# Nine attention transposes of units 8 to 12 done by SyncE's transfers instead of TensorE, and one output copy done by ScalarE instead of VectorE

## The chip, the cores and the metric

The kernel runs on one core of one Trainium2 chip. The metric is the device time of one execution in microseconds; lower is better. Before the change the median of three runs is 290.44 us (289.84 to 291.09).

## The reference

A sliding-window attention over 8 batches of 8 heads, 576 positions and 64 dimensions is followed by a feed-forward block over the resulting 4608 tokens of width 512, with a hidden width of 2048 and a gelu approximated by a sigmoid. The output is float32.

```python
def _attn_ref(q, k, v):
    ...
    window = 32
    scale = 1.0 / np.sqrt(D)
    scores = scale * np.matmul(q, k.transpose(0, 1, 3, 2))
    pos = np.arange(S)
    mask = np.abs(pos[:, None] - pos[None, :]) <= window
    scores = np.where(mask, scores, -1000000000.0)
    ...                                   # softmax over the last axis
    return np.matmul(attn, v).astype(np.float32)

def _moe_ref(x, w_in, w_out):
    h = x @ w_in
    g = h * (1.0 / (1.0 + np.exp(-1.702 * h)))
    return (g @ w_out).astype(np.float32)
```

## The kernel before

The 4608 tokens are cut into 36 units of 128 keys and into nine tiles of 512 tokens, four units to a tile. Everything is written out by hand in program order: each engine executes its instructions in the order in which the program issues them, and waits on semaphores that the framework sets from the buffers used.

A unit passes through these steps. GpSimd's transfers load its queries, keys and values and turn them into bfloat16 (`fetch`, `load_kq`, `load_v`; the queries and keys go to the staging buffers `qst` and `kst`, five of each). Queries and keys are transposed so that the head dimension lies on the partitions (`qT`, `kT`, seven buffers of each, handed out by `place`). TensorE multiplies them (`scores`), ScalarE takes the exponential (line 256), VectorE applies the band mask (`band`), TensorE multiplies by the values (`values`), VectorE divides (`norm`), and the result `x` is transposed again into `xT`, the right operand of the first layer. The values are also needed shifted by half a unit; GpSimd makes that copy (`odd_v`, lines 209 and 210).

How queries and keys are transposed depends on the unit. Units 0 to 7 are transposed on TensorE by two routines of their own. Keys 8 to 12 and queries 8 to 11 are transposed on TensorE by `T_pe`: four transposes of 128x128 for each, three operands at a time into the two banks "t", and ScalarE copies each to its place. From query 12 and key 13 on, `turn` has SyncE issue a transfer that transposes (`T_dma`, line 223). The transposes of `x` are also SyncE's transfers from tile 3 on (line 306); the output stores stand in the same queue (line 453). At most eight transfers of a queue are under way: each waits for the one eight before it.

The feed-forward block of tile 0 is computed plainly (`layer1_plain`, `layer2_plain`); the later tiles use seven products in place of eight for a 2x2 block product. For the first layer that is `l1_group`, four groups to a tile. A group's seven products are issued in the order P1, P7, P6, P2, P5, P4, P3 into four banks A, C, B, E. ScalarE copies A to B, and C to `s7`, after P1 and P7; P6 adds to B; VectorE writes E = B + s7 (line 432) and, after P5 has added to B, C = B + s7 (line 438); then come four gelus (line 419). Between the products, `fill` puts in matmuls of the second layer of the tile before and work for VectorE: sums of weights (`w1_sums`, `w2_sums`, lines 335 and 346) and sums of the hidden layer (`g_sums`, lines 366 to 369).

The change concerns the first layer of tile 1, `first_layer1`, from 48 to 70 us of the span. Its fills hold the plain second layer of tile 0: two halves of 32 matmuls each, whose two banks LA and LB are copied out at the last of their 16 matmuls (line 475). In this stage the transposes of `T_pe` stand after P7 of groups 1, 2 and 3, and GpSimd loads units 12 to 15. Ahead of it, at the end of `opening`, stand the scores of unit 7, which still read the keys at the start of unit 8 from a buffer of the opening.

Of the kernel before, what the change touches and what calls it, by code (L numbers as in the profile page):

```python
# [16 lines left out]
BF16 = mybir.dt.bfloat16  # L17
# [9 lines left out]
class _Kernel:  # L27
# [191 lines left out]
    def T_dma(self, c, u):  # L219
# [1 line left out]
            return  # L221
        src = self.stage.pop((c, u))
        self.nc.sync.dma_start_transpose(self.place(c, u), src.rearrange("p h d -> p (h d)"))

    def T_pe(self, which, eng):

        tp = self.bank("t", [128, 4, 4, 128], BF16, "tp")
        which = [(x[0], int(x[1:])) for x in which]
        for i, (c, u) in enumerate(which):
            src = self.stage.pop((c, u)).rearrange("p h d -> p (h d)")  # L230
            for hp in range(4):
                self.nc.tensor.transpose(tp[:, i, hp, :], src[:, 128 * hp:128 * hp + 128], self.ident)  # L232
        for i, x in enumerate(which):
            self.copy(eng, self.place(*x), tp[:, i])

    def scores(self, u, tag):
        kT, q = self.kT[u], self.qT[u]
# [224 lines left out]
    def layer2_plain(self, t, pr):  # L464

        st = {}

        def part(i, f):
            if not st:
                st.update({j: self.bank("L" + "AB"[j], name="o") for j in range(2)})  # L470
                st["o"] = self.sb("o_sb", [128, 2, self.DM], F32, 2)
            lo = 256 * i + 128 * pr
            self.mm(st[i], self.g[t][:, f, lo:lo + 128], self.w2[:, f, :], start=(f == 0))
            if f == 15:
                self.copy((self.nc.vector, self.nc.scalar)[i * pr], st["o"][:, i, :], st[i])
                if i == 1:
                    self.store(t, pr, st["o"])

        return [lambda i=i, f=f: part(i, f) for q in range(8) for i in range(2) for f in (2 * q, 2 * q + 1)]
# [82 lines left out]
    def opening(self):  # L562

        nc, dve, act, pool = self.nc, self.nc.vector, self.nc.scalar, self.nc.gpsimd
        self.setup()
        dve.memset(self.idle, 0.0)
        dve.memset(self.spark, 0.0)
        for t in self.ve:
            dve.memset(t[:, :, self.D:], 1.0)
        self.load_first("k", 0)  # L570
        self.load_first("q", 0)
        make_identity(nc, self.ident)
        act.activation(self.spark, self.spark, AF.Exp)
        for u in (0, 1, 2):
            self.load_v(u)
        self.load_w1(0)
        self.setup_mask()
        self.load_first("k", 1)
        self.load_first("q", 1)
        self.cut_mask()  # L580
        self.load_w1(1)
        self.load_v(3)
        self.load_v(4)
        self.load_w1(2)
        self.load_four("k")
        self.load_four("q")
        self.load_w1(3)
        dve.tensor_copy(self.identh, self.ident)
        self.keep_busy(20, "E")
        self.T_first("k", 0, "AC", (dve, act))  # L590
        self.keep_busy(6, "E")
        self.T_first("q", 0, ("LA", "LB"), (dve, act))
        self.keep_busy(4, "E")
        for u in (5, 6):
            self.load_v(u)
        self.load_w2(0)
        for u in (7, 8):
            self.load_v(u)
        for c in (1, 2, 3):
            self.load_w2(c)  # L600
        self.load_kq("k", 8)
        self.scores(0, "t")
        self.scores(1, "AC")
        self.odd_v(0, dve)
        self.odd_v(1, dve)
        self.keep_busy(10, "E")
        self.band(0)
        self.band(1)
        self.values(0, "t")
        self.values(1, "AC")  # L610
        self.norm(0)
        self.norm(1)
        self.keep_busy(6, "E")
        self.x_T(0, "LA", act)
        self.keep_busy(4, "E")
        self.x_T(1, "LB", act)
        self.T_first("k", 1, "AC", (dve, dve))
        h, n, gelus = [], [0], []

        def l1(half, *ds):  # L620
            for d in ds:
                self.layer1_plain(0, d, half, h[n[0] % len(h)])
                n[0] += 1

        self.layer1_plain(0, 0, 0, "B", gelus)
        self.T_first("q", 1, ("LA", "LB"), (dve, act))
        self.layer1_plain(0, 1, 0, "E", gelus)
        self.odd_v(2, dve)
        self.odd_v(3, dve)
        h[:] = ["LB", "B", "E"]  # L630
        self.scores(2, "t")
        self.scores(3, "AC")
        self.layer1_plain(0, 2, 0, "LA", gelus)
        self.layer1_plain(0, 3, 0, "LB", gelus)
        self.do(gelus)
        self.band(2)
        self.band(3)
        self.values(2, "t")
        self.norm(2)
        self.values(3, "AC")  # L640
        self.norm(3)
        self.x_T2(2, "A", dve)
        l1(0, 4)
        dve.tensor_copy(self.k_first, self.kT[0][:, :, 0:64])
        dve.tensor_copy(self.v_first, self.ve[0][0:64])
        for u in (8, 9, 10, 11):
            self.fetch(u)
        l1(1, 0, 1)
        halo = self.kT[4]
        self.T_four("k", "AC", (dve, dve))  # L650
        dve.tensor_copy(self.kT[4][:, :, 0:64], halo)
        l1(1, 2, 3)
        l1(0, 5)
        self.T_four("q", "AC", (dve, act))
        l1(1, 4, 5)
        self.odd_v(4, dve)
        self.scores(4, "t")
        self.scores(5, "AC")
        for i in (3, 1, 2, 4):
            self.w1_sums((i,), 0)  # L660
        self.odd_v(5, dve)
        for d, tag in ((6, "B"), (7, "E")):
            self.layer1_plain(0, d, 0, tag, gelus)
        self.do(self.l2, 3)
        self.scores(6, "t")
        self.do(self.l2, 3)
        self.scores(7, "AC")
        self.do(gelus)
        self.do(self.l2, 2)
        self.band(4)  # L670
        self.band(5)
        self.odd_v(6, dve)
        self.odd_v(7, dve)
        self.band(6)
        self.values(4, "t")
        self.norm(4)
        self.band(7)
        self.values(5, "AC")
        self.norm(5)
        self.do(self.l2, 8)  # L680
        self.values(6, "t")
        self.norm(6)
        self.values(7, "AC")
        self.norm(7)
        h[:] = "BE"
        n[0] = 0
        for i in (3, 1):
            self.w1_sums((i,), 1)
        l1(1, 6, 7)
        self.x_T2(4, "A", act)  # L690
        self.do(self.l2, 4)
        self.x_T2(6, "t", dve)
        self.do(self.l2, 4)
# [147 lines left out]
    def first_layer1(self):  # L841

        dv = [lambda i=i: self.w1_sums((i,), 1) for i in (2, 4)]
        for n in range(4):
            if n == 3:
                self.turn(12)
                self.turn(13)
            self.odd_v(8 + n, self.nc.gpsimd)
            self.fetch(12 + n)

            def fill(i):
                self.do(self.l2, {1: 1, 7: 1, 2: 3, 4: 3}[i])
                self.do(dv, {1: 2, 7: 1, 2: 0, 4: 2}[i] if n else 0)
                if i == 7 and n:
                    self.T_pe([("k8", "q8", "k9"), ("q9", "k10", "q10"), ("k11", "q11", "k12")][n - 1], self.nc.scalar)

            self.l1_group(1, n, fill, lambda i: self.do(dv, 1))
            dv += self.g_sums(1, 2 * n, 2)
            if n in (0, 1):
                dv += [lambda i=i, j=j: self.w2_sums((i,), j) for i in ((3, 1), (2, 4))[n] for j in range(2)]  # L860
        return dv
# [46 lines left out]
```

## Time and profile before

| | |
|---|---|
| median of three runs | 290.44 us |
| lowest, highest run | 289.84, 291.09 us |
| span of the profiled execution, first to last instruction | 287.4 us |
| granted TensorE clock over the span | 1.000 |
| VectorE, ScalarE, GpSimd busy share of the span | 75%, 68%, 44% |
| transfers | 37.63 MB in 148074 packets |

The profile is of one execution. The page gives its span, not a time of its own; the runs' median lies 3.0 us above that span. Busy shares are averages over all stages, so a question about one place is asked of the rows of that place: a timeline gives start and length in us of each instruction, or of a run of equal ones, with their count, and in brackets how long the engine was idle before it and what it then waited for. The chain of waits lists the work that ended last, followed back from the end.

### The profile page before, as it was taken

The page shows a single profiled execution, that of the slowest core. Times are in us where ns is not written, and L with a number is a line of the kernel's source. Part 1 is how long each engine was busy: PE and PEld are TensorE (multiplying, and loading weights), DVE is VectorE, ACT ScalarE, POOL GpSimd, SP SyncE. Part 2 cuts the span into 40 slices and gives each one's busy share as a digit, 9 for nine tenths or more (in the row PEclk, how much of TensorE's full clock was granted, in tenths as well). Part 3 has the DMA queues.
Part 4 walks back from the last instruction along what each step waited for, and adds up shares of the span by engine and source line. Part 5 has one row for each costly group of instructions (what it writes and reads, how often), then busy time and mean ns, then how long its engine had stood idle before and what let it go on. Part 6 is the DMA issues. An engine that isn't in the chain of part 4 may idle for free.

```text
span 287.4 us, 9107 instructions
## 1 busy us (share of the span) xinstructions
PE 274.7 (96%) x3762; PEld 227.1 (79%) x3762; DVE 216.9 (75%) x501; ACT 194.0 (68%) x340; POOL 127.3 (44%) x192
## 2 busy tenths in 40 slices
PE   7878999999999997999999999999999999999995
PEld 5666857776777885888788888888888888888884
DVE  1756898897887975798779887988797878946731
ACT  2455784789787767676967696679668965558421
POOL 8964448798599746456345826360210000000000
PEclk9999999999999999999999999999999999999999
DMA  8999999999999999999999999998432150401023
GB/s 94 186 192 197 184 204 156 190 116 140 168 141 148 175 142 173 138 203 144 188 97 181 161 168 105 173 135 146 95 77 45 69 112 0 94 2 73 2 92 130
DMA packets 148074, 37.63 MB, mean 131 GB/s; under 512 B 134976, under 2 KB 143680, under 8 KB 148032
## 3 DMA queue, kind: packets, MB, share of 16 engines
q0 software_dynamic: 104464, 18.42, 92.3%
q1 hardware_dynamic: 43120, 18.10, 36.0%
q8 instruction: 29, 0.48, 0.7%
q10 hardware_dynamic: 448, 0.52, 0.6%
q14 instruction: 13, 0.11, 0.1%
HBM read 36.83 MB, written 9.44 MB: 161 GB/s over the span
## 4 chain that ended last, share of the span: by engine, by line
PE 81%; DMA 5%; DVE 5%; ACT 3%; POOL 2%; issue 2%; DVEq 0%; ACTq 0%; POOLq 0%
PE h L70 38%; PE o L70 34%; PE pv L70 3%; DMA xT<-x 3%; PE sc L70 2%; DMA kq<-in_k_dram 2%; DVE x L294 2%; ACT p L256 1%; PE tp L322 1%; POOL ve L199 1%; ACT L256 1%; DVE p L264 1%; PE tp L189 1%; PE tp L232 1%; ACT g L419 1%
## 5 line engine op out<-in xcount | busy, mean ns | idle before, releaser
L419 ACT ACTIVATE g<-h 128x512 f16<-128x512 f32 x128 | 72.1, 598 | 35.8 <-PE h L70 35.0
L70 PEld LDWEIGHTS <-g 128*128 128x128 f16 x576 | 54.4, 98 | 11.4 <-issue 1.8
L70 PEld LDWEIGHTS <-a 128*128 128x128 f16 x512 | 49.1, 97 | 12.7 <-DVE xs L354 2.1
L70 PE MATMUL h<-xs,a 128*128 128x256 f16 x384 | 57.6, 272 | 1.2 <-DVE xs L354 0.9
L70 PE MATMUL o<-w,g 128*128 128x256 f16 (+1 forms) x320 | 55.3, 294 | 0.9 <-issue 0.8
L70 PEld LDWEIGHTS <-w 128*128 128x128 f16 x512 | 49.1, 98 | 7.8 <-issue 1.2
L70 PE MATMUL h<-xT,w 128*128 128x256 f16 x384 | 54.0, 273 | 1.1 <-issue 1.0
L199 POOL DMA_DIRECT2D ve<-in_v_dram x40 | 34.0, 855 | 40.7 <-issue 33.7
L70 PEld LDWEIGHTS <-gs 128*128 128x128 f16 x384 | 36.8, 98 | 5.2 <-issue 0.4
L256 ACT ACTIVATE p<-sc 128x512 bf16<-128x512 f32 x72 | 36.6, 619 | 3.2 <-PE sc L70 3.2
L70 PE MATMUL o<-b,gs 128*128 128x256 f16 x256 | 37.8, 273 | 1.0 <-issue 0.5
L70 PE MATMUL o<-b,g 128*128 128x256 f16 x256 | 37.3, 273 | 0.0
L432 DVE TENSOR_TENSOR h<-h,s 128x512 f32<-128x512 f32 x32 | 22.3, 698 | 18.2 <-PE h L70 18.2
L131 POOL DMA_DIRECT2D qst<-in_q_dram x35 | 28.1, 805 | 5.5 <-DMA w<-in_moe_w_out_dram 3.2
L131 POOL DMA_DIRECT2D kst<-in_k_dram x31 | 26.4, 854 | 8.5 <-DMA ve<-in_v_dram 2.6
L67 ACT COPY h<-h 128x512 f32<-128x512 f32 x32 | 18.6, 581 | 16.6 <-PE h L70 16.2
L294 DVE TENSOR_TENSOR x<-pv,rec 128x256 f16<-128x256 f32 (+1 forms) x53 | 27.6, 520 | 1.8
L438 DVE TENSOR_TENSOR h<-h,s 128x512 f32<-128x512 f32 x32 | 22.4, 700 | 5.1 <-PE h L70 4.6
L264 DVE TENSOR_TENSOR p<-p,mask 128x1024 bf16<-128x1024 bf16 x36 | 24.6, 685 | 0.9 <-ACT p L256 0.8
L209 POOL COPY vo<-ve 64x264 int32<-64x264 int32 x28 | 13.4, 480 | 24.9 <-PE pv L70 23.8
L67 ACT COPY s<-h 128x512 f32<-128x512 f32 x32 | 19.1, 596 | 3.0 <-PE h L70 1.8
L70 PE MATMUL h<-xs,w 128*128 128x256 f16 x128 | 19.2, 273 | 0.0
(85 smaller groups left out, 361.1 us busy)
## 6 DMA issues: line engine op xcount, KB each, us to landing
out_dram<-o_sb SPq DMA_DIRECT2D x33, 256.0 KB, 3.9
ve<-in_v_dram POOLq DMA_DIRECT2D x32, 128.0 KB, 6.3
kst<-in_k_dram POOLq DMA_DIRECT2D x25, 128.0 KB, 6.8
qst<-in_q_dram POOLq DMA_DIRECT2D x21, 128.0 KB, 6.1
w<-in_moe_w_in_dram POOLq DMA_DIRECT2D x4, 512.0 KB, 8.9
w<-in_moe_w_out_dram POOLq DMA_DIRECT2D x4, 512.0 KB, 13.4
qst<-in_q_dram POOLq DMA_DIRECT2D x7, 96.0 KB, 5.5
kq<-in_q_dram POOLq DMA_DIRECT2D x2, 256.0 KB, 5.9
```

Of the source, the lines that this page charges most:

```text
L67: (eng.copy if eng is self.nc.scalar else eng.tensor_copy)(out, in_)
L70: self.nc.tensor.matmul(out, lhsT, rhs, start=start, stop=stop, skip_group_check=True)
L131: self.nc.gpsimd.dma_start(t[off:off + n], src[b, :, s:s + n, :].rearrange("h s d -> s h d"))
L189: self.nc.tensor.transpose(tp[64 * (h % 2):64 * (h % 2) + 64, h // 2, j, :], src[:, 4 * i + h, j, :], self.ident)
L199: self.nc.gpsimd.dma_start(t[off:off + n, :, :self.D], self.v[b, :, s:s + n, :].rearrange("h s d -> s h d"))
L209: eng.tensor_copy(words(vo[64:128]), words(self.ve[u % 9][64:128]))
L256: self.nc.scalar.activation(p[:, eo].rearrange("k h s -> k (h s)"), sc[eo], AF.Exp, scale=self.scale)
L264: (eng or self.nc.vector).tensor_mul(pv, pv, msk.to_broadcast([128, 8, 2, SQ]))
L294: dve.tensor_mul(x[:, 4 * at:4 * (at + n), :].rearrange("p (b h) d -> p b h d", b=n), acc[:, :, :, :D], r.to_broadcast([128, n, 4, D]))
L419: act.activation(g[:, f, 256 * half:256 * half + 256], bank.rearrange("p (i n) -> p i n", i=2), AF.Gelu_apprx_sigmoid)
L432: dve.tensor_add(e, b, s7)
L438: dve.tensor_add(c, b, s7)
```

## The change

The routine `T_pe` and its calls go. Keys 8 to 10 and queries 8 and 9 are transposed by SyncE's transfers, issued behind the scores of unit 7; query 10 and key 11 at the start of group 1 of `first_layer1`, query 11 and key 12 at the start of group 2. In the plain second layer of tile 0, the copy of the second bank goes to ScalarE in both halves; before, it did so in the second half alone.

```diff
-    def T_pe(self, which, eng):
-
-        tp = self.bank("t", [128, 4, 4, 128], BF16, "tp")
-        which = [(x[0], int(x[1:])) for x in which]
-        for i, (c, u) in enumerate(which):
-            src = self.stage.pop((c, u)).rearrange("p h d -> p (h d)")
-            for hp in range(4):
-                self.nc.tensor.transpose(tp[:, i, hp, :], src[:, 128 * hp:128 * hp + 128], self.ident)
-        for i, x in enumerate(which):
-            self.copy(eng, self.place(*x), tp[:, i])
...
             if f == 15:
-                self.copy((self.nc.vector, self.nc.scalar)[i * pr], st["o"][:, i, :], st[i])
+                self.copy((self.nc.vector, self.nc.scalar)[i], st["o"][:, i, :], st[i])
...
         self.scores(7, "AC")
+        self.T_dma("k", 8)
+        for u in (8, 9):
+            self.turn(u)
         self.do(gelus)
...
         for n in range(4):
+            if n in (1, 2):
+                self.turn(9 + n)
             if n == 3:
                 self.turn(12)
                 self.turn(13)
...
-                if i == 7 and n:
-                    self.T_pe([("k8", "q8", "k9"), ("q9", "k10", "q10"), ("k11", "q11", "k12")][n - 1], self.nc.scalar)
```

`turn(u)` transposes the queries of unit u and the keys of unit u + 1.

## The prediction

> **What bounds the kernel now.** I read the page's busy shares and chain of waits first, then that chain between 44 and 76 us, where the edited instructions stand, then the timelines of VectorE, ScalarE and GpSimd there, and last SyncE's transposes.
>
> ```profile
> span 287.4 us, 9107 instructions
> PE 274.7 (96%) x3762; PEld 227.1 (79%) x3762; DVE 216.9 (75%) x501; ACT 194.0 (68%) x340; POOL 127.3 (44%) x192
> PE 81%; DMA 5%; DVE 5%; ACT 3%; POOL 2%; issue 2%; DVEq 0%; ACTq 0%; POOLq 0%
> ```
>
> TensorE is busy 96% of the span and carries 81% of the chain. Work taken off it is therefore worth something, but only as far as no other engine becomes late at that place. The 287.4 us are the span of the profiled execution; the median of the runs, 290.44, lies 3.0 us above it, outside the instructions, which the change does not touch. So a gain inside the span is subtracted from 290.44.
>
> The chain in the stage that changes (start, length, what):
>
> ```profile
> 51.36 0.70 DVE h L438
> 52.06 0.69 DVE a L336
> 52.75 0.61 DVE o_sb L67
> 53.36 0.04 issue
> 53.40 0.38 PE o L70
> ...
> 54.43 0.67 PE tp L232 x12
> ...
> 59.88 0.67 PE tp L232 x12
> ...
> 65.48 0.67 PE tp L232 x12
> ...
> 68.58 1.68 ACT g L419 x3
> ...
> 70.28 1.28 ACT L256
> ...
> 75.44 0.60 PE o L70 x4
> ```
>
> The three blocks of twelve transposes lie on the chain, 0.67 us each. Behind the last of the four groups of tile 1's first layer the chain passes to ScalarE at 68.58 (gelus, table load, exponentials) and only comes back to TensorE at 75.44. So what the change is worth here is how much earlier the three gelus at 68.58 start; the rest of the kernel follows at the same distance.
>
> **What is taken away: 36 transposes and 9 copies.** TensorE loses 3 x 0.67 = 2.0 us. That is the ceiling. Inside a group I call the seven products P1 to P7 as the kernel does; the order is P1, P7, (transposes), P6, P2, P5, P4, P3. P6 accumulates into bank B, which ScalarE must first have seeded with a copy of bank A, behind the last gelu of the group before. P5 may overwrite what VectorE's sum at L432 reads, and P3 what the sum at L438 reads. TensorE first, then ScalarE and VectorE:
>
> ```profile
> 54.94 0.60 PE L70 MATMUL h<-xs,a 128*128 128x256 f16 x4
> 60.39 0.60 PE L70 MATMUL h<-xs,a 128*128 128x256 f16 x4
> 62.06 0.60 PE L70 MATMUL h<-xs,a 128*128 128x256 f16 x4
> ```
> ```profile
> 51.80 1.68 ACT L419 ACTIVATE g<-h 128x512 f16<-128x512 f32 x3 [0.92 <-PE h L70]
> 53.51 0.57 ACT L67 COPY h<-h 128x512 f32<-128x512 f32 x1
> ...
> 59.25 0.57 ACT L67 COPY h<-h 128x512 f32<-128x512 f32 x1
> ```
> ```profile
> 57.10 0.70 DVE L438 TENSOR_TENSOR h<-h,s 128x512 f32<-128x512 f32 x1 [0.43 <-PE h L70]
> 57.70 2.90 DVE L346 TENSOR_TENSOR b<-w 128x1024 f16<-128x1024 f16 x4
> 60.53 0.41 DVE L366 TENSOR_TENSOR gs<-g 128x512 f16<-128x512 f16 x1
> 60.97 0.42 DVE L367 TENSOR_TENSOR g<-g 128x512 f16<-128x512 f16 x1
> 61.32 0.69 DVE L432 TENSOR_TENSOR h<-h,s 128x512 f32<-128x512 f32 x1
> ...
> 62.70 0.70 DVE L438 TENSOR_TENSOR h<-h,s 128x512 f32<-128x512 f32 x1 [0.36 <-PE h L70]
> ...
> 66.70 0.70 DVE L432 TENSOR_TENSOR h<-h,s 128x512 f32<-128x512 f32 x1 [0.24 <-PE h L70]
> ```
>
> Seed: in group 2 the copy ends at 59.25 + 0.57 = 59.82, P6 starts at 60.39. Without the transposes P6 can start 0.04 after the copy, so at most 60.39 - 59.86 = 0.53 of the 0.67 is to be had per group from ScalarE's side.
>
> VectorE: the row at 61.32 has no idle time before it. From the sum at 57.10 to the one at 61.32 VectorE works without a pause, 4.22 us, and P5 at 62.06 starts 0.74 behind that sum: in group 2 TensorE already waits for VectorE. Taking transposes off TensorE does not shorten this stretch. It is fixed to the P5 before it: the sum at L438 starts 0.64 after P5 (62.70 - 62.06), so P5 of group 1 stands at 57.10 - 0.64 = 56.46. Likewise 62.70 to 66.70 is 4.00 with 0.24 idle, 3.76 of work.
>
> **What is moved: one copy, from VectorE to ScalarE.** The second operand of the pick is now the bank alone, so of tile 0's first pair of output banks the second copy changes engine; the other copies stay. On VectorE it stood from 53.3 to 53.9 and hid behind the gelus that the next sum waits for anyway. On ScalarE it comes between the first and second gelu of the trio at 51.80, ahead of the seed of group 1. A copy of that size is the 0.57 above. The seed ends at 53.51 + 0.57 + 0.57 = 54.65, and P6 of group 1 starts at 54.69 instead of 54.94: 0.25 gained of 0.67. TensorE's own wait until 53.40 for the copy at 52.75 stays, as that is the first bank; it is covered by this wait.
>
> The sum, group by group:
> - Group 1: P5 at 56.46 - 0.25 = 56.21; L438 at 56.85.
> - Group 2: L432 at 56.85 + 4.22 = 61.07, P5 at 61.81, gain 0.25; L438 at 62.45.
> - Group 3: L432 at 62.45 + 3.76 = 66.21, P5 at 66.95. Before, P5 stood 1.07 ahead of the gelus at 68.58 (0.43 for itself, 0.63 from P4 to its gelu), at 67.51. Gain 0.56.
>
> One term of it is not fixed. The four L346 sums overlap GpSimd's copies of the odd value blocks:
>
> ```profile
> 54.95 1.38 POOL L131 DMA_DIRECT2D kst<-in_k_dram  x2 [1.91 <-PE tp L232]
> ...
> 57.74 0.92 POOL L209 COPY vo<-ve 64x264 int32<-64x264 int32 x1
> 58.71 0.75 POOL L210 COPY vo<-ve 64x264 int32<-64x264 int32 x1
> ...
> 62.57 0.41 POOL L209 COPY vo<-ve 64x264 int32<-64x264 int32 x1
> ...
> 74.86 0.56 POOL L209 COPY vo<-ve 64x264 int32<-64x264 int32 x1 [4.19 <-PE pv L70]
> ```
> ```profile
> L346 DVE TENSOR_TENSOR b<-w x4: 679/781/891, 57.7 to 59.9; 128x1024 f16<-128x1024 f16 x4
> L346 DVE TENSOR_TENSOR b<-w,b x2: 678/678/679, 63.6 to 64.2; 128x1024 f16<-128x1024 f16 x2
> ```
>
> Where they overlap both are slow: 0.92 against 0.41 on GpSimd, a median of 781 against 678 ns on VectorE. GpSimd waits 1.91 us at 54.95 for the first transposes, which free key unit 8's buffer. Now SyncE frees it before GpSimd comes to it at 53.04, so these copies move to about 55.8, off the four sums. If each of those takes 678, the stretch is 4 x 0.10 = 0.4 us shorter: P5 of group 2 at 61.4, of group 3 at 66.5, gain 0.99. Later copies then fall on other sums and give part of it back. Between 0.56 and 0.99 I take 0.8.
>
> **What is added: nine transposes on SyncE's queue**, the first five at a place where nothing stands in that queue before its first output store.
>
> ```profile
> 42.99 0.88 POOL L131 DMA_DIRECT2D kst<-in_k_dram  x1 [2.44 <-DMA w<-in_moe_w_out_dram]
> ```
> ```profile
> kst<-in_k_dram POOLq DMA_DIRECT2D x25, 128.0 KB, 6.8
> ```
> ```profile
> L223 SPq DMA_TRANSPOSE qT<-qst x24: 1188/1215/2119, 56.6 to 210.0; - x24
> L223 SPq DMA_TRANSPOSE kT<-kst x23: 1191/1352/2633, 58.9 to 208.6; - x23
> ...
> DMA to landing us min/median/max: 2.4/6.3/10.0
> ```
>
> Each holds SyncE's queue 1.2 to 1.35 us and lands after 6.3 in the median, 10.0 at most. The first five wait for the loads of keys 8 to 10 and queries 8 and 9, whose last is the one issued at 42.99 us and lands 6.8 later, near 50, so they are out by 51 to 53 us; the store behind them, which waits for VectorE's copy that ends at 53.36, is about on time. The other four stand behind it, are out by about 60 and land by 70 even at 10.0. Unit 8 is used first, after the last group, where its transposes have been done for over 10 us; units 10 and 11 come several us later. Behind them in the queue the transposes of units 12 and on start at 59 to 60 rather than 56.65, again far ahead of their use. So on SyncE I cost them at nothing: the cover is 10 us, and gone only if a landing took over 15. What they take from other transfers is the open cost. From below it is 0; from above, each holds the transfers 1.2 us as it holds the queue: 9 x 1.2 = 10.8 us between 44 and 62. GpSimd, which issues the loads, has 1.91 + 4.19 = 6.1 us of waits in that stage to absorb it. I take 0, since that is the nearer end for anything used before 75 us, and keep the rest for a rival.
>
> Sum: -0.8 us, 290.44 to 289.6.
>
> **Rivals.**
>
> *TensorE's whole saving arrives.* If VectorE's sums, rid of the overlap, and ScalarE, rid of nine copies, keep pace, 2.0 us go: 288.4. For it: the blocks are on the chain three times. Against it: the row at 61.32 with no idle, and the 0.57 us copy ahead of group 1's seed. I give it 0.22.
>
> *Nothing arrives.* If the moved copy costs ScalarE the full 0.67 in group 1 and VectorE's stretches do not get shorter, the gain is 0.3 (only the idle 0.24 ahead of group 3's sum goes): 290.1. Chance 0.08.
>
> *The transfers crowd, and it gets slower.* Place: the x transposes that tile 3's sums wait for.
>
> ```profile
> 103.43 8.78 DMA xT<-x
> ```
>
> There the chain is a transfer for 8.78 us, in a stage crowded with loads, transposes and stores. Of 10.8 us of added transfer work, 6.1 are absorbed in GpSimd's waits; 4.7 would still be queued at 75 us, when the next loads are due. If half of that is made good by 103, the x transposes land 2.4 us later: 289.6 + 2.4 = 292.0. It decides once more than 0.8 us of backlog is left at 103. Against it: most of the transposes overlap loads, and GpSimd waits 4.19 us at 74.86 anyhow. Chance 0.25.
>
> [...]
>
> **How the numbers follow.** Forecast 0.45, whole saving 0.22, nothing 0.08, slower 0.25. A measurement of this kernel tells about 0.5% (1.45 us) from no change: faster means under 289.0, slower over 291.9. The forecast's own range, 289.4 to 289.9, and "nothing" lie within, 0.53; faster 0.22; slower 0.25. The range goes from 288.3 to 292.0, the two outer cases.
>
> **What would show it.** Right: no L232 rows; P6 of groups 2 and 3 starting just behind ScalarE's seed; L432 of group 2 with no idle before it; GpSimd's copies at about 56; the gelus of group 3 near 67.8; nothing late at 103. Wrong: gelus of group 3 near 66.6 (whole saving), or x transposes landing over 9 us after their issue, with TensorE idle beyond today's at 112; or TensorE waiting at unit 8's scores for a transpose.

## The result: the changed kernel is slower

| | before | after |
|---|---|---|
| median of the runs | 290.14 us (4 runs, 287.54 to 291.09) | 293.04 us (4 runs, 290.71 to 293.78) |
| profiled execution: time, span | span 287.4 us | 292.96 us, span 291.1 us |
| granted clock over that span | 1.000 | 0.982 |

The ratio after to before is 1.0118, 95% interval 1.0069 to 1.0167 (the two medians alone give 1.0100). The forecast was 289.6 us in a range of 288.3 to 292.0; the result lies above the range. The profile of experiment 1 below is of the slowest of its six runs, 295.00 us, which the ratio of that experiment leaves out.

From the page of the changed kernel, the lines that answer to those of before, and the granted clock in 40 slices of 7.3 us:

```profile
span 291.1 us, 9044 instructions
PE 277.5 (95%) x3726; PEld 228.3 (78%) x3726; DVE 217.2 (75%) x500; ACT 189.9 (65%) x332; POOL 125.7 (43%) x192
PEclk9997999999986999999999999999999999999999
```

TensorE has 36 instructions fewer, as forecast, but is busy 277.5 us where it was 274.7: the same products took longer in two places, where the clock falls to 7, 8 and 6 tenths (four products that took 0.61 us take 1.04, below). The chain of waits in the stretch that begins with the changed stage is this (in the changed kernel a line behind the old `T_pe` stands 13 lower, down to the added transfers; 419 is the old 432, 406 the old 419):

```profile
54.03 0.58 ACT o_sb L67
...
67.78 0.62 DVE h L419
...
69.51 1.68 ACT g L406 x3
...
77.77 0.98 PE o L70 x8
79.11 7.27 DMA kT<-kst
86.42 0.64 PE sc L70 x15
```

Ahead of the gelus at 69.51 the moved copy (54.03) and VectorE's sums, the last at 67.78, stand where the three blocks of transposes stood. From the gelus to 77.77 it is the chain of before. Then comes a piece that it did not have: for 7.27 us the chain is one transposing transfer, of key unit 16, and TensorE goes on behind it at 86.42. TensorE's timeline there, after and then before:

```profile
83.49 0.24 PE L70 MATMUL sc<-qT,kT 64*64 64x64 bf16 x2
86.42 0.64 PE L70 MATMUL sc<-qT,kT 64*64 64x64 bf16 x22 [2.69 <-DMA kT<-kst]
86.99 1.04 PE L70 MATMUL h<-xT,w 128*128 128x256 f16 x4
...
111.30 0.70 PE L70 MATMUL sc<-qT,kT 64*64 64x64 bf16 x48
...
139.11 0.70 PE L70 MATMUL sc<-qT,kT 64*64 64x64 bf16 x48
```
```profile
82.56 0.45 PE L70 MATMUL sc<-qT,kT 64*64 64x64 bf16 x24
82.94 0.61 PE L70 MATMUL h<-xT,w 128*128 128x256 f16 x4
...
104.94 0.70 PE L70 MATMUL sc<-qT,kT 64*64 64x64 bf16 x48
...
135.02 0.70 PE L70 MATMUL sc<-qT,kT 64*64 64x64 bf16 x48
```

The scores of unit 15 issue two matmuls at 83.49 and the other 22 after 2.69 us of idle time. The four products behind them take 1.04 us where they took 0.61. The windows show why, after and then before (columns: window, its length, busy time of PE, PEld, DVE, ACT, POOL with the number of instructions, granted clock, DMA share, GB/s):

```profile
23.50:27.00 3.50, 3.23 (x20) 2.54 (x21) 1.75 (x6) 0.78 (x2) 1.62 (x3) 0.52 1.44 196
81.70:85.10 3.40, 1.79 (x44) 1.20 (x38) 2.56 (x7) 2.35 (x5) 3.40 (x4) 0.99 1.97 206
85.10:91.90 6.80, 5.48 (x46) 4.01 (x47) 2.14 (x5) 3.52 (x5) 5.35 (x9) 0.50 1.95 182
104.00:120.00 16.00, 16.00 (x253) 13.39 (x252) 13.04 (x30) 13.22 (x23) 6.82 (x10) 1.00 1.89 170
```
```profile
23.50:27.00 3.50, 3.14 (x31) 2.65 (x32) 1.80 (x6) 1.64 (x4) 1.19 (x2) 1.00 1.45 195
81.70:85.10 3.40, 3.16 (x57) 2.38 (x51) 2.58 (x7) 3.40 (x7) 3.30 (x5) 1.00 2.24 155
85.10:91.90 6.80, 6.67 (x85) 5.41 (x84) 5.35 (x12) 5.29 (x10) 6.66 (x10) 1.00 2.52 136
104.00:120.00 16.00, 14.16 (x235) 11.48 (x233) 11.68 (x29) 12.04 (x20) 8.34 (x13) 1.00 1.84 156
```

Behind the wait the granted clock is 0.50 for 6.8 us, and 46 matmuls were done there and not 85. TensorE works there from 86.42 to 91.90; by the granted clock these 5.48 us hold 5.48 x 0.50 = 2.74 us of full-speed work, so by this estimate the wait costs about as much again as its own 2.69 us.

Where the 3.7 us of span come from is read off four marks on these timelines. The seed copy of group 0 of tile 1 (the first copy h<-h of that stage) starts at 48.55 before and 50.01 after: +1.46, lost before any edited instruction. From there to the last three gelus, 68.58 and 69.51, it is 20.03 and 19.50: -0.53. From them to the start of unit 15's scores, 82.56 and 83.49, it is the same 14.0. From these to the scores at 104.94 and 111.30, 22.4 and 27.8: +5.4, which is the wait and the lost clock, 2.69 + 2.74. From these to the next tile's, at 135.02 and 139.11, 30.1 and 27.8: -2.3, given back, because before TensorE stood idle 1.84 of the 16 us from 104 to 120 (0.94 of them ahead of 112.78, for VectorE's sum over an x whose transpose the chain runs through for 8.78 us from 103.43), and after it is busy 16.00 of the 16. The rest of the span is 0.4 shorter. The sum, +1.46 - 0.53 + 5.4 - 2.3 - 0.4, is +3.6, against 3.7.

The +1.46 is not the change's. It goes with the half-clock stretch at 23.5 to 27.0 (0.52), which the profiled execution of before does not show (1.00), but that of the same kernel in experiment 11 does (0.51), with its seed copy at 50.14 (below).

### The profile page after: what moved, and what is told of

It reads as the page before. It is cut to its first block, busy times and chain, and to the rows that moved or that the text cites. A ratio compares the mean times of both kernels' runs of the same rounds, so it can differ in the third digit from the quotient of the medians.

```text
span 291.1 us, 9044 instructions
## 1 busy us (share of the span) xinstructions
PE 277.5 (95%) x3726; PEld 228.3 (78%) x3726; DVE 217.2 (75%) x500; ACT 189.9 (65%) x332; POOL 125.7 (43%) x192
## 3 DMA queue, kind: packets, MB, share of 16 engines
q1 hardware_dynamic: 48016, 19.28, 40.6%
## 4 chain that ended last, share of the span: by engine, by line
PE 80%; DMA 5%; DVE 5%; ACT 4%; POOL 3%; issue 2%; ACTq 0%; POOLq 0%
PE h L70 38%; PE o L70 35%; PE pv L70 3%; DMA w<-in_moe_w_in_dram 3%; PE sc L70 3%; DMA kT<-kst 2%; ACT p L243 1%; DVE x L281 1%; DVE h L419 1%; POOL ve L199 1%; ACT g L406 1%; ACT L243 1%; POOL kq L143 1%; PE tp L309 1%; PE tp L189 1%
## 5 line engine op out<-in xcount | busy, mean ns | idle before, releaser
L70 PEld LDWEIGHTS <-a 128*128 128x128 f16 x512 | 49.9, 98 | 13.7 <-issue 3.4
L70 PE MATMUL h<-xs,a 128*128 128x256 f16 x384 | 58.5, 275 | 1.2 <-DVE h L419 0.6
L70 PE MATMUL h<-xT,w 128*128 128x256 f16 x384 | 56.0, 280 | 1.2 <-issue 1.0
L70 PEld LDWEIGHTS <-w 128*128 128x128 f16 x512 | 50.1, 100 | 8.8 <-issue 1.2
L425 DVE TENSOR_TENSOR h<-h,s 128x512 f32<-128x512 f32 x32 | 22.4, 700 | 5.5 <-PE h L70 5.1
L209 POOL COPY vo<-ve 64x264 int32<-64x264 int32 x28 | 12.9, 459 | 23.5 <-PE pv L70 22.4
```

The lines of the kernel that those rows point to most:

```text
L70: self.nc.tensor.matmul(out, lhsT, rhs, start=start, stop=stop, skip_group_check=True)
L209: eng.tensor_copy(words(vo[64:128]), words(self.ve[u % 9][64:128]))
L425: dve.tensor_add(c, b, s7)
```

## The experiments

The ratios compare each kernel with runs of the kernel before on the same chip. Experiment 11, the kernel before compared with itself, gave 1.0045 [1.0009, 1.0080], so a ratio up to about 1.008 does not count as a loss here. What is read from a trace is read from one execution.

**1. The transposes moved, the copy left on VectorE.**

```diff
-                self.copy((self.nc.vector, self.nc.scalar)[i], st["o"][:, i, :], st[i])
+                self.copy((self.nc.vector, self.nc.scalar)[i * pr], st["o"][:, i, :], st[i])
```

> The nine transposes on SyncE, but the output copy on VectorE as before. Theory A (late key: the nine added transfers crowd the loads, the load of key unit 16 is issued some 3 us later, its transpose lands near 86 us, and TensorE stands idle about 2.7 us at the scores of unit 15, after which its granted clock drops): the idle time at those scores stays, 2 to 4 us, with granted clock under 1 behind it; time 1.005 to 1.015 of before. Rival B (the moved copy on ScalarE is what costs): no stall to speak of, time 0.995 to 1.000 of before. By both, group 1's seed comes about 0.4 us sooner against group 0 than in the changed kernel.

Measured: 293.15 us, 1.0126 [1.0073, 1.018]. The stage, seed copy to last gelus, takes 18.97 us (before 20.03, after 19.50). So the transposes alone bring 1.06 us there, the moved copy costs 0.53 of it, and the whole is as slow as the full change. The waits between 70 and 92 us of this kernel's trace show the same place (columns: engine and line, what it waited for, us in total, times, longest):

```profile
PE sc L70 <- DMA qT<-qst: 3.9, 1, 3.9
PE sc L70 <- DMA kT<-kst: 1.2, 1, 1.2
```

The loss is there without the moved copy: it is the transposes'.

**2 and 8. Only the copy moved**, the routine `T_pe` and its calls kept; run twice.

```diff
-                self.copy((self.nc.vector, self.nc.scalar)[i * pr], st["o"][:, i, :], st[i])
+                self.copy((self.nc.vector, self.nc.scalar)[i], st["o"][:, i, :], st[i])
```

> Only the output copy moved to ScalarE, the transposes on TensorE as before. Theory A: within 0.3% of before, TensorE does not wait for a key at unit 15's scores. Rival B: 1.008 to 1.015 of before.

> The copy alone on ScalarE once more, since it measured 1.008 where its trace showed no loss in the stage. If the loss is real, 1.005 to 1.012 of before and a place in the trace where at least 1 us is lost; if it comes from how the windows of the granted clock fall in each execution, within 0.997 to 1.004.

Measured: 291.37 us, 1.0083 [1.0046, 1.012], and 290.64 us, 1.0069 [1.0032, 1.0106]. The stage takes 20.10 and 20.00 us (20.03 before), and no score waits for a key. Both ratios are above the 0.3% expected of a copy that costs nothing, the first at the low end of what rival B expected, and neither is clear of the control's interval. Experiment 4 below has the moved copy too and measures 1.0010. Whether the copy costs anything by itself is not settled. The mean granted clocks of the two sets of runs are spread alike, 0.987 to 0.999 and 0.988 to 1.000, and nothing here shows what decides where in an execution the clock falls.

**3. The whole change, but queries 15 and keys 16 transposed on TensorE**, behind the scores of unit 14.

```diff
-        self.turn(15)
...
+        tp = self.bank("A", [128, 2, 4, 128], BF16, "tp")
+        self.T_one("q", 15, tp[:, 0], act)
+        self.T_one("k", 16, tp[:, 1], act)
```

> The changed kernel, but the queries of unit 15 and the keys of unit 16 transposed on TensorE, behind unit 14's scores, so that their landing does not count; eight more transposes there, 0.45 us. Theory A: the idle time of 2.7 us at unit 15's scores and the low clock behind it go or fall under 1 us, and the time comes to 0.993 to 1.002 of before. Rival C (the crowding costs all along, that stall is only where it shows, and another transfer is late next, at tile 3's sums): the stall moves and the time stays 1.005 to 1.015 of before.

Measured: 291.18 us, 1.0083 [1.0056, 1.0111], above what theory A expected and within the range of rival C. TensorE still waits 1.56 us there and the clock falls again, to 8 tenths in the page's slice of 79.5 to 86.7 us: four products at 86.05 take 1.04 us, as behind the wait of the change. But this wait is the experiment's own. The load of key 16, issued at 72.31, landed after 6.5 us, at 78.8, and the wait ends at 84.19, just behind ScalarE's copy of query 15 (83.49 to 84.14), which lies in the same bank as the transposes of key 16. So this experiment does not decide between the two; a fall of the clock behind a wait of 1.56 us that is no transfer's is what it adds.

**4. The nine transfers kept, as plain copies of the same 128 KB.** The scores of units 8 to 12 are then formed from data that was not transposed.

```diff
         src = self.stage.pop((c, u))
+        if u < 12 + (c == "k"):
+            self.nc.sync.dma_start(self.place(c, u).rearrange("p h d -> p (h d)"), src.rearrange("p h d -> p (h d)"))
+            return
```

> The changed kernel with the nine transfers of units 8 to 12 as plain copies of the same 128 KB instead of transposes; the scores of these units are therefore computed from untransposed data. Theory A with the transposing as the cause: the loads of the stage land as before (median about 5 us between 50 and 60 us instead of 10), key 16 is in time, no stall at unit 15's scores, time 0.990 to 0.998 of before. Rival D (any nine more transfers, or the order on SyncE's queue, are the cause): the stall stays, over 1.005 of before.

Measured: 288.84 us, 1.0010 [0.9972, 1.0047]. The wait is gone and the clock is 1.00 from 85.1 to 91.9. From unit 15's scores to the next tile's it is 84.16 to 106.55, 22.4 us as before. The same number of transfers, of the same size, in the same places of the queue, cost nothing that these runs can tell once they do not transpose. (The gain that theory A expected with it, 0.990 to 0.998, does not show either.) What they leave to the loads is seen from the transfers that moved between 50 and 60 us: before, after, and with plain copies (q0 carries GpSimd's loads, q1 SyncE's transfers; packets, MB, time as a share of 16 engines; then KB each and us to landing):

```profile
q0 software_dynamic: 8573, 1.08, 171.1%
q1 hardware_dynamic: 832, 0.66, 21.0%
...
kst<-in_k_dram POOLq DMA_DIRECT2D x1, 128.0 KB, 5.4
...
qst<-in_q_dram POOLq DMA_DIRECT2D x1, 128.0 KB, 4.5
```
```profile
q0 software_dynamic: 7078, 0.89, 142.0%
q1 hardware_dynamic: 2378, 0.65, 52.4%
...
kst<-in_k_dram POOLq DMA_DIRECT2D x1, 128.0 KB, 9.9
...
qst<-in_q_dram POOLq DMA_DIRECT2D x1, 128.0 KB, 12.1
```
```profile
q0 software_dynamic: 8953, 1.13, 176.6%
q1 hardware_dynamic: 774, 0.89, 29.1%
...
kst<-in_k_dram POOLq DMA_DIRECT2D x2, 128.0 KB, 8.0
...
qst<-in_q_dram POOLq DMA_DIRECT2D x1, 128.0 KB, 6.6
```

The changed kernel's loads bring in 0.89 MB in these 10 us, against 1.08 before and 1.13 with plain copies. The landings are not quite as before with plain copies: 8.0 and 6.6 us, between the 5.4 and 4.5 of before and the 9.9 and 12.1 of the change. Over the whole span q1 has 43120 packets before, 48016 after and 44416 here: (48016 - 43120) / 9 = 544 packets for one transposing transfer, (44416 - 43120) / 9 = 144 for a plain one of the same bytes.

**5 and 6. Three, or five, of the nine moved**, the others left on TensorE in groups 2 and 3 (three moved) or group 3 (five moved), and the copy on VectorE.

```diff
         self.T_dma("k", 8)
-        for u in (8, 9):
-            self.turn(u)
+        self.turn(8)
...
-            if n in (1, 2):
-                self.turn(9 + n)
...
+                if i == 7 and n > 1:
+                    self.T_pe([("q9", "k10", "q10"), ("k11", "q11", "k12")][n - 2], self.nc.scalar)
```

With five moved, `self.turn(9)` follows `self.turn(8)`, and one call in group 3 takes q10, k11, q11 and k12.

> Keys 8 and 9 and queries 8 on SyncE (three transposes), the other six on TensorE in groups 2 and 3 as before, the copy on VectorE as before. Theory A (late key by crowding of transfers): three are few enough, GpSimd issues the load of key 16 within 1.5 us of before counted from the first group, no idle time over 0.5 us at unit 15's scores, stage from the first seed copy to the last gelu trio 0.4 to 0.7 us shorter than the 20.0 of before; time 0.993 to 1.000 of before. Rival C (any added transposing transfer costs): over 1.004.

> Keys 8 to 10 and queries 8 and 9 on SyncE (five transposes), four on TensorE in group 3, the copy on VectorE as before. Theory A: between; the load of key 16 some 1.5 to 2.5 us later than before, idle time at unit 15's scores 0 to 1.5 us, stage 0.5 to 1.0 us shorter; time 0.996 to 1.006 of before. Rival C: over 1.006.

Measured: three moved 289.06 us, 0.9990 [0.9951, 1.0029]; five moved 290.55 us, 1.0075 [1.0043, 1.0107]. In neither profile does a score wait for a key. Between 50 and 60 us the loads with three moved carry 1.08 MB, as before; with five, 0.88, as after. So the crowding is there with five already, and by itself it does not yet make TensorE wait in that execution; the time of five moved is nevertheless above the 0.996 to 1.006 expected, and the trace, of one of its quicker runs (289.36 us), shows no place for it. With three it is absent, and the stage takes 19.28 us, 0.75 less than before; the runs do not show that as a gain.

**7. The kernel before, with nine extra transposing transfers** at the same places, into a buffer that nothing reads; TensorE's transposes all stay.

```diff
+    def T_extra(self, c, u):
+        d = self.sb("extra", [128, 4, 128], BF16, 3)
+        self.nc.sync.dma_start_transpose(d, self.stage[c, u].rearrange("p h d -> p (h d)"))
...
+        for c, u in (("k", 8), ("q", 8), ("k", 9), ("q", 9), ("k", 10)):
+            self.T_extra(c, u)
...
+            if n in (1, 2):
+                self.T_extra("q", 9 + n)
+                self.T_extra("k", 10 + n)
```

> The kernel before, with nine additional transposes on SyncE at the places of the change, from the same staging buffers into a buffer that nothing reads; all its own work stays, on TensorE too. Theory A: the crowding alone makes the loss, so TensorE stands idle 1 to 4 us at unit 15's scores and the time is 1.006 to 1.020 of before. Rival B (it is TensorE or ScalarE, not the transfers): 0.998 to 1.003.

Measured: 295.64 us, 1.0247 [1.0195, 1.03]. GpSimd's and then TensorE's timeline of this kernel:

```profile
78.17 0.87 POOL L131 DMA_DIRECT2D kst<-in_k_dram  x1 [9.65 <-DMA kT<-kst]
```
```profile
87.72 0.54 PE L70 MATMUL sc<-qT,kT 64*64 64x64 bf16 x16 [5.24 <-DMA kT<-kst]
```

Nothing was taken off TensorE and no result depends on the added transfers, yet the wait for key 16 appears, at the scores of the same unit, followed again by half a clock (0.50 from 86.2 to 93.0). Wait and time are above what was expected. Here the extra transfers hold the queue until 68.3, so that the transposes of units 12 on come later too, and the load of key 16 waited 9.65 us, which its row puts down to one of these transposes of keys; why that load hangs on it is not settled.

**9. The kernel before, with tile 3's four transposes of x on TensorE.** These are what the chain of before runs through at 103.43.

```diff
-                self.x_T(u + n - 1)
...
-                    self.x_T(u + n)
...
+                if t == 2 and n in (1, 3) and i == 4:
+                    self.x_T2(u + n - 1, "t", self.nc.scalar)
```

> The other direction: the kernel before, with the four x transposes of tile 3 (units 12 to 15), whose landing the chain waited for at 103 us, done on TensorE in pairs instead of by SyncE. Theory A (SyncE's transposes are what is late where transfers crowd): the wait before tile 3's sums goes, TensorE idles under 0.5 us between 104 and 120 instead of 1.8, 0.9 us of transposes come to TensorE; time 0.992 to 0.999 of before. If transfers do not matter there: 1.002 to 1.006.

Measured: 290.79 us, 1.0075 [1.0043, 1.0107]. In the profile, which is of the slowest run (293.00 us), TensorE is busy 15.31 of the 16 us from 104 to 120 (14.16 before); its one wait there, 0.66 us, is for ScalarE's copy of the transposed x. The time does not fall, and lies above both ranges expected: taking the wait for the transfer away brings nothing that these runs can tell.

**10. Experiments 5 and 9 together.** Its diff is the two above.

> Both: keys 8 and 9 and queries 8 on SyncE early (the kernel of three moved), and tile 3's x transposes on TensorE. Theory A: 0.990 to 0.998 of before, the best so far. If each is worth nothing: 0.998 to 1.004.

Measured: 290.56 us, 1.0069 [1.0036, 1.0101]. Expected as the best version, and it is not.

**11. The kernel before, compared with itself.**

> The kernel before itself, against itself, to see what a ratio of this size is worth after the copy alone measured 1.007 and 1.008 with no loss in its stage. If ratios of such size come from the comparison: outside 0.996 to 1.004. If the comparison is sound: inside it.

Measured: 289.83 against 288.60 us, 1.0045 [1.0009, 1.0080]. That is a bias of the comparison of about half a per cent, of unknown cause. The full change (1.0118, 1.0115) and experiment 1 (1.0126) lie above this interval, though the lower ends of their own intervals (1.0069, 1.0060, 1.0073) lie within it; experiment 7 (1.0247) is clear of it; experiments 4 and 5 lie below or at its low end; 2, 3, 6, 8, 9 and 10 are not told from it. Its profile has the half clock in the opening:

```profile
23.50:27.00 3.50, 2.92 (x18) 2.34 (x19) 2.03 (x7) 0.41 (x2) 1.41 (x2) 0.51 1.44 197
```

So the +1.46 us that the changed kernel's profile loses ahead of the stage occurs without the change. Of the profiles here those of before and of experiments 2, 6, 7 and 8 do not have a stretch of half clock in the opening, the others do; whether the change makes it more frequent is open.

**12. The full change once more.** No edit.

> The changed kernel once more, with twelve runs, since the kernel before measured 1.0045 against itself and the first result stands on four runs. Theory A: key 16's load is again issued some 3 us later than before counted from the first seed copy, TensorE idles 2 to 5 us at unit 15's scores, the granted clock halves behind it; ratio 1.008 to 1.018, above the control's interval. If the loss was the comparison's: 1.001 to 1.008, and no idle time at unit 15's scores.

Measured: 292.23 us, 1.0115 [1.006, 1.0171]. In this execution TensorE's wait is shorter:

```profile
84.98 0.47 PE L70 MATMUL sc<-qT,kT 64*64 64x64 bf16 x22 [1.28 <-DMA kT<-kst]
```

It is below the 2 to 5 us expected, and the clock is half for one stretch, 85.2 to 88.7 (0.53 over the window from 85.10 to 88.70), half as long as the 6.8 us of the change.

The granted clocks of all the runs point the same way. One such stretch, 3.4 us at half clock in a span of 290, lowers the mean clock by 0.006, so one, two and three of them would give 0.994, 0.988 and 0.982. That is an estimate; the profiles agree with it: the control's, with 0.994, has one, that of experiment 12, with 0.988, two, and the changed kernel's, with 0.982, 3.4 us in the opening and 6.8 behind the wait. All ten runs of the changed kernel lie at 0.994 or below. Of the 98 runs of the kernel before that the experiments were compared with, 61 lie at 0.998 or above, of the twelve with plain copies 7, but of the control's own twelve only 4.

The profiles together order by one number: how late after group 0's seed copy the keys of unit 16 are there. The scores of unit 15 begin 33.3 to 34.2 us after that copy, experiment 1 aside.

| kernel | load of key 16 issued, us after the seed copy | its transpose issued | landed | wait of unit 15's scores, us | ratio |
|---|---|---|---|---|---|
| 5, three moved | 17.3 | 23.3 | 26.5 | 0 | 0.9990 |
| 4, plain copies | 15.7 | 24.3 | 28.1 | 0 | 1.0010 |
| before | 19.5 | 24.7 | 28.2 | 0 | 1 |
| 6, five moved | 19.8 | 25.5 | 28.9 | 0 | 1.0075 |
| 12, the change again | 20.2 | 28.0 | 35.0 | 1.28 | 1.0115 |
| the change | 21.3 | 29.1 | 36.4 | 2.69 | 1.0118 |
| 1, copy kept | 23.7 | 31.6 | 39.4 | 3.89 + 1.20 | 1.0126 |
| 7, nine extra | 30.2 | 34.6 | 39.7 | 5.24 | 1.0247 |

In experiments 2, 8, 9, 10 and 11 it lands at 27.7 to 30.6 and no score waits for it, with ratios of 1.0045 to 1.0083; so the order holds for the waits, and for the times only above about 1.008. In experiment 1 the scores wait for query 15 first.

None of these profiles has a landing between 30.6 and 35.0. The transfer's own time goes with that gap: where it is issued ahead of GpSimd's next batch of loads (73.25 against 75.84 before) it lands after 2.5 to 3.8 us, in all nine profiles without a wait; where it comes behind the start of that batch (79.11 against 76.77 in the change) it lands after 5.1 to 7.8, in all four with one. Before and in the change:

```profile
kT<-kst SPq DMA_TRANSPOSE x1, 3.5
```
```profile
kT<-kst SPq DMA_TRANSPOSE x1, 7.3
```

## Why the prediction was wrong

**What is taken away, what is moved: right, and close in size.** The stage gained 0.53 us; the steps gave 0.56 to 0.99 and 0.8 was taken. VectorE's timeline after:

```profile
58.41 0.70 DVE L425 TENSOR_TENSOR h<-h,s 128x512 f32<-128x512 f32 x1 [0.43 <-PE h L70]
59.02 2.48 DVE L333 TENSOR_TENSOR b<-w 128x1024 f16<-128x1024 f16 x4
...
62.22 0.69 DVE L419 TENSOR_TENSOR h<-h,s 128x512 f32<-128x512 f32 x1
...
63.60 0.70 DVE L425 TENSOR_TENSOR h<-h,s 128x512 f32<-128x512 f32 x1 [0.37 <-PE h L70]
...
64.54 1.28 DVE L333 TENSOR_TENSOR b<-w,b 128x1024 f16<-128x1024 f16 x2
65.74 1.70 DVE L334 TENSOR_TENSOR b<-w,b 128x1024 f16<-128x1024 f16 x2
...
67.70 0.68 DVE L419 TENSOR_TENSOR h<-h,s 128x512 f32<-128x512 f32 x1
```

- Group 1: ScalarE's seed now ends at 55.63 + 0.57 = 56.20 and P6 starts at 56.26, 0.11 late; forecast 54.69, which is 56.15 with the 1.46 us by which this execution is later.
- Group 2: VectorE is the bound, with no idle time before the sum at 62.22. Its stretch is 62.22 - 58.41 = 3.81, 0.41 less than the 4.22 of before; forecast 0.4 less, because GpSimd's copies leave the four sums of line 333. They do: they stand at 57.83, and the four sums take 2.48 instead of 2.90.
- Group 3: 67.70 - 63.60 = 4.10, where the forecast of 0.56 had 3.76. GpSimd's next copies now stand at 65.48 and 66.15 and fall on the two sums of line 334, which take 1.70 where the two before them take 1.28. The prediction had named this and left 0.2 of the 0.99 for it. It took 0.34 (4.10 - 3.76); with the 0.11 of group 1 that is the 0.46 missing from 0.99.

The rival "the whole saving arrives" falls: even with the copy kept, experiment 1, the stage gains 1.06 and not 2.0. "Nothing arrives", priced at 0.3 us, falls too: the stage took 19.50 and, in experiment 12, 19.48 us, against 20.03 and, in the control, 20.05.

**What is added: this is the step that failed.** The prediction set the nine transposes' cost to nothing, on the ground that their own results are not needed for 10 us, and that the transposes behind them come "again far ahead of their use". The first half held: no score of units 8 to 12 waits, and the first output store is issued at 54.86, on time. The second did not. SyncE after and before:

```profile
79.11 1.21 SPq L223 DMA_TRANSPOSE kT<-kst  x1
```
```profile
73.25 2.04 SPq L223 DMA_TRANSPOSE kT<-kst  x1
```

Unit 12's queries go out at 64.00 (forecast 59 to 60), and key 16 at 79.11 instead of 73.25. It lands 7.27 us behind its issue, at 86.38, three microseconds after the scores of unit 15 begin to need it; before it landed after 3.5 us, at 76.8. Counted from the seed copy that is 8.2 us later: 1.8 from the issue of its load, 1.1 from that load's landing (6.2 against 5.1), 1.5 from standing behind query 15 in SyncE's queue, and 3.8 from its own landing, among the next loads. The first of these begins with GpSimd, whose timeline after is:

```profile
57.11 0.68 POOL L199 DMA_DIRECT2D ve<-in_v_dram  x1 [1.97 <-DVE gs L355]
...
60.97 0.89 POOL L131 DMA_DIRECT2D kst<-in_k_dram  x1 [0.80 <-DMA ve<-in_v_dram]
64.56 0.88 POOL L199 DMA_DIRECT2D ve<-in_v_dram  x1 [2.71 <-DVE h L425]
...
71.28 0.89 POOL L131 DMA_DIRECT2D kst<-in_k_dram  x1
```

In both traces at most 8 of GpSimd's 121 loads are under way at once (of SyncE's transfers at most 7), none starts less than 0.28 us behind the landing of the one eight places ahead, and those under way in this stage now take 9 to 12 us to land instead of 4.5 to 5.4. So GpSimd waits 1.97, 0.80 and 2.71 us before loads that it used to issue without a pause. (Two of these rows name VectorE. The landings say otherwise: the loads that stand eight places ahead were issued at 47.53, 50.12 and 51.87 and landed after 9.0, 10.2 and 12.1 us, at 56.5, 60.3 and 64.0, and GpSimd goes on about 0.6 us behind each, at 57.11, 60.97 and 64.56.) The prediction counted 6.1 us of GpSimd's waits as room that absorbs the transfers. It was not room: the wait of 1.91 us did go, and the slower landings put 5.5 us of new ones in its place, ahead of the load of key 16; the other, 4.19 us, ends at 74.86, behind that load, and could absorb nothing ahead of it.

**The rival "the transfers crowd, and it gets slower" is what happened, at another place and another price.** The prediction looked for it at 103 us, where the chain of before already ran through a transfer. There the changed kernel is better: TensorE, idle 1.84 us from 104 to 120 before, is busy 16.00 of the 16. It came 20 us earlier, at the scores of unit 15. The price, 2.4 us, is near the wait (2.69 and 1.28 in the two executions) by chance, since it was worked out for another transfer, and it lacked the clock: 6.8 us at 0.50 behind it, so that the stretch grew by 5.4 us and gave 2.3 back. By a chance of 0.25 and an upper end of 292.0 it was both too unlikely and too cheap. What would have found it in the profile of before is the load at 68.00 and its transpose at 73.25, against scores at 82.56: with the prediction's own median of 6.3 us to landing (79.6) 3 us of room, with the 3.5 us that this transfer took 5.8. By the median that is the shortest room of the queries and keys of units 12 to 15, and far from "far ahead". The prediction measured the room of the moved transposes only.

**The time outside the span** was read as 3.0 us, the median less the span. In the changed kernel's profiled execution it is 292.96 - 291.1 = 1.9. The execution profiled before was thus about 1 us quicker than the median that the gain was taken from. What a longer one can have besides, a stretch of half clock (37 of the 98 runs of this kernel beside the experiments lie below 0.998), was not in the rows.

A transposing transfer and a plain copy of the same bytes were not equal here, beside other traffic: the transposing form took 544 packets and left the loads 0.89 MB in 10 us, the plain form 144 packets and 1.13 MB; those issued between 50 and 60 us landed after 8.0 us as transposes and 6.0 to 6.3 as copies; and the two kernels differ by 1.0118 to 1.0010 in time.

**What stays open:** whether the moved copy costs anything beyond its 0.53 us in the stage; what makes five moved transposes 1.0075 where the trace shows no wait; why the kernel before compared with itself gives 1.0045; and whether the opening's half clock depends on anything but chance. No version here beats the kernel before.

## What to carry to other kernels

When work moves to a transfer queue, look for the room of what stands behind it and beside it, not only of what was moved: for each later load, its issue, its landing, the transfer that needs it, and the first instruction that waits, against the least slack in the profile of before. Idle time of the engine that issues loads was no reserve here: the loads themselves got slower, and 5.5 us of new waits for landings stood where 1.91 us had gone. A transfer's room is not what it has in a quiet moment: once this one slipped among the next loads it took longer itself, 7.3 us for 3.5. A wait of TensorE is to be priced with the clock that the trace shows behind it: here 0.50 for 6.8 us, by estimate 2.74 us more on a wait of 2.69.

## What the runs showed of the hardware

The granted clock was 0.50 for 6.8 us after the wait of 2.69 us, 0.53 over 3.6 us after the wait of 1.28 us (experiment 12), and 0.51 over 3.5 us in the opening in one execution of the kernel before (experiment 11), where it was 1.00 in another. In the 3.4 us ahead of the fall in the changed kernel TensorE was busy 1.79 us (the row of 81.70 to 85.10), and the pause that begins in them lasts 2.69 us; in the same 3.4 us it was busy 3.16 us before and 3.01 with plain copies, and the clock stayed at 1.00. In the 3.4 us from 20.10 to 23.50, ahead of the stretch in the opening, it was busy 1.40 us in the changed kernel and 1.23 in the control, where the clock fell, and 1.54 before, where it did not. What decides the fall was not shown.

A transfer that transposes 128 KB within SBUF held its queue 1.2 to 1.35 us in the median before (1.25 to 1.38 in the changed kernel) and took 544 packets, and nine of them among other loads took those loads' time to landing from 5.4 and 4.5 us to 9.9 and 12.1. Nine plain copies of the same bytes, at 144 packets each, took it to 8.0 and 6.6 and cost no time that the runs can tell.
